# A tuned attention-and-experts kernel on one core: row remainders loaded in parts, and set issue times for the loads of later batches

## The chip, the cores and the metric

The kernel runs on one core of one Trainium2 chip. The metric is the device time of one execution in microseconds (us). The kernel before takes 508.6 us. All outputs are right. In each run the device time is about 1.8 us more than the span of its profile (508.58 against 506.8, say), so times are compared with times and spans with spans.

Engines are named as in the profile: PE is TensorE's matmuls, PEld its weight loads, ACT is ScalarE, DVE is VectorE, POOL is GpSimd and SP is SyncE. The program gives each of the five a queue of instructions of its own, and semaphores in it hold an instruction back until its inputs are there.

## The reference

Linear attention for 8 batches of 8 heads (576 rows, 64 columns), then a mixture of 4 experts on the 4608 rows that come out.

```python
phi(x) = np.where(x > 0, x, np.exp(x) - 1.0) + 1.0
q_p, k_p = phi(q), phi(k)                      # (8, 8, 576, 64)
kv  = einsum('bhsd,bhde->...', k_p, v)         # summed over the rows
z   = sum(k_p, axis=2)
x   = (q_p @ kv) / (q_p . z + 1e-06)           # then (4608, 512)
p   = domain_probs / (domain_probs.sum(-1) + 1e-9)
out = sum over e of  p[:, e] * (relu(x @ w1[e]) @ w2[e])   # D 512, F 1024
```

(The first two einsums are shortened to what matters here.)

## The kernel before

576 rows are 4 x 128 + 64. The 64 rows left over, the *row remainders*, are loaded for all heads of a batch at once. Attention goes by *pairs* of heads: `kv` sums over the rows of k and v, so it needs the remainders of k and v, but the outputs of the first 512 rows do not need the remainder of q.

The first 512 rows of batch 0 are run through the experts plainly as the weights arrive (the *ramp*, up to about 85 us). The other 4096 rows are 64 *units*, each 14 products of 8 or 4 matmuls, among which the attention of batches 2 to 7 is mixed in (until about 400 us).

The order of every engine's queue is made by a small planner inside the kernel. It goes through an assumed time line, takes on each engine the ready operation with the lowest `pri` (on POOL the next one as the program lists them), and writes the queues in the order found. A load lands, so the planner assumes, 2.0 us plus a moving time after its issue. `after` is the earliest assumed time of an operation. It is no time on the chip: on the chip it only settles where an instruction stands in its queue.

```python
    # Plan.order()
    start[n] = max(t, at[n])                  # at[n] begins as the operation's "after"
    free[e] = done = start[n] + o["dur"]
    if o["move"]:                             # a DMA
        mover = max(done + 1.2, mover) + o["move"]
        done = mover + 0.8                    # assumed landing
    ...
    def load_rest(b, queue, pri):             # the remainders: k, v and q together
        for i, (t, o) in enumerate(((k, kqr[rs, 0]), (v, vr[rs]), (q, kqr[rs, 1]))):
            dma(queue, pri, o, t[b, :, NT:S]..., (("str", par, i),), 0.75, ...)

    def rest_maps(b, pe_mode, pri):           # one exponential for k and q
        pl.add("ACT", 1.05, pri, lambda: nc.scalar.activation(er[rs], kqr[rs], AF.Exp),
               r=(s_[0], s_[2]), w=ek)
        ...
    # the start
    load_pair(0, 0, "SP", 0)
    load_rest(0, "POOL", 0)
    load_pair(0, 1, "POOL", 0)
    load_w1(0, (0,))
    ...
    def batch(b):                             # batches 2 to 7, mixed into the units
        due = U(8 * (b - 1)) - 8              # U(n) = 84 + 6.4 n, the assumed start of unit n
        for pr in range(DC):
            t = due - (DC - pr) * 2 * TU
            load_pair(b, pr, "SP", t - 12)    # only a priority: goes as soon as its buffer is free
            if pr == 0:
                load_rest(b, "SP", t - 12)
                rest_maps(b, False, t - 6)
            attention(b, pr, False, t, 1.7)
```

## Time and profile before

508.58 us (median of 3 runs, 508.37 to 508.6). The profiled run itself took 510.41 us, 1.8 us more than that median.

| where | time TensorE loses, us |
|---|---|
| 0 to 12 us | 11.5 |
| 12 to 34 us | 11.5 |
| 34 to 85 us | 1.3 |
| 85 to 115 us | 3.9 |
| 115 to 450 us | 1.0 |
| after 500 us | 7.5 |

*Lost* is the length of the stretch less the time that its matmuls take at the spacing of an unhindered stream (0.216 us for 512 columns, 0.109 for 256, 0.056 for 128). In all, the matmuls need 472.0 of the 508.6 us, so TensorE is the bound and 36.6 us is all that any reordering could win. It is a better measure here than the busy share, since matmuls overlap: the view of windows has PE busy for 484.1 us of the first 508.

Busy time of each engine by stage, from the view of windows of the kernel before. After the stretch and its length come the engines' busy times with instruction counts, then the granted clock (1.00 is full), the mean busy share of the DMA engines and GB/s:

```profile
0.00:12.00 12.00, 1.54 (x10) 0.97 (x10) 6.20 (x19) 6.30 (x10) 10.04 (x20) 1.00 0.86 226
12.00:34.00 22.00, 17.39 (x98) 9.29 (x99) 16.66 (x51) 13.52 (x29) 14.98 (x23) 0.92 1.15 223
...
60.00:85.00 25.00, 25.00 (x139) 12.27 (x138) 21.33 (x49) 18.29 (x36) 1.44 (x3) 1.00 0.88 175
85.00:115.00 30.00, 28.31 (x360) 24.19 (x358) 26.93 (x69) 24.77 (x48) 0.00 (x0) 1.00 0.99 213
115.00:260.00 145.00, 144.80 (x1992) 137.37 (x1990) 131.84 (x344) 120.73 (x230) 0.00 (x0) 1.00 0.65 146
```

(No clock is on record before 21.5 us in this trace; the 1.00 of the first stretch rests on none.)

The start, from the timeline of the kernel before (start, length, engine, line, operation, output and inputs; in brackets the idle time before it and what ended it):

```profile
9.21 1.06 ACT L317 ACTIVATE ek<-kqr 64x1024 f16<-64x1024 f32 x1 [0.30 <-DMA kqr<-in_q_dram]
...
10.77 0.29 PE L403 MATMUL l2b<-vpr,kqpr 128*128 128x130 f16 x1 [4.99 <-DVE kqpr L315]
...
16.73 1.44 PE L537 MATMUL l1b<-s,w 128*128 128x512 f16 x3 [0.15 <-ACT s L532]
...
24.02 0.27 DVE L289 TENSOR_REDUCE prs<-p 128x32 f32<-128x128 f32 x1
...
26.89 0.64 PE L527 MATMUL l2b<-identh,x 128*128 128x128 f16 x4 [0.80 <-DVE x L440]
...
28.21 1.36 PE L537 MATMUL l1b<-s,w 128*128 128x512 f16 x3 [0.67 <-ACT s L532]
```

One exponential for both remainders starts at 9.21 us, when the q remainder has landed; TensorE waits 5 us for the mapped k remainder until 10.77. The first expert matmul comes at 16.73. The norm of the last pair stands behind the probabilities (from 24.02) on DVE, and the last chunk of the first layer starts at 28.21, after two idle spells.

```profile
kq<-in_q_dram SPq DMA_DIRECT2D x18, 256.0 KB, 3.1
...
kq<-in_k_dram SPq DMA_DIRECT2D x17, 256.0 KB, 3.2
```

Almost nothing: 1.2 us. A load goes out as soon as its buffer is free (at the issue of a q load 1.7 other transfers from SP are in flight on average, counted from the trace), and is there when its turn comes.

### The profile page before, as it was taken

To read this page: it belongs to the slowest core of one execution; us is meant where nothing else is said; L and a number is where in the kernel's file an instruction comes from. 1 tells how busy PE (TensorE), PEld (TensorE's weight loads), DVE (VectorE), ACT (ScalarE), POOL (GpSimd) and SP (SyncE) were. 2 spreads that over 40 slices of the span, in tenths; PEclk is the share of its full clock that TensorE was granted. 3 is DMA by queue.
4 is the path that set the end of the run, shared out by engine and by line. 5 is a ranking of instruction groups with operands and counts; after the bars stand their busy time and mean duration, and the time that the engine had idled before them with its cause. 6 is when DMAs were issued, how large, how long until landed. Compare 5 with 4: busy or idle time off the path is not lost.

```text
span 508.6 us, 14922 instructions
## 1 busy us (share of the span) xinstructions
PE 484.1 (95%) x6008; PEld 425.0 (84%) x6008; DVE 410.6 (81%) x1035; ACT 367.1 (72%) x685; POOL 42.6 (8%) x68
## 2 busy tenths in 40 slices
PE   1889999999999999999999999999999999999994
PEld 0534454889999999999999999999999999999993
DVE  5867897889998989898988989799868676666754
ACT  5636658887987699768977897778666766666640
POOL 8756500000000000000000000000000000000000
PEclk9989999999999999999999999999999999999999
DMA  8999988995775678555665565645322432323311
GB/s 233 227 232 225 262 164 188 234 201 136 162 182 120 138 145 177 121 137 129 175 112 136 124 147 141 108 113 105 95 43 75 54 84 44 84 48 80 51 35 43
DMA packets 124006, 67.51 MB, mean 133 GB/s; under 512 B 94480, under 2 KB 117776, under 8 KB 123936
## 3 DMA queue, kind: packets, MB, share of 16 engines
q1 hardware_dynamic: 115216, 51.79, 46.9%
q0 software_dynamic: 8720, 14.76, 13.7%
q8 instruction: 47, 0.77, 0.7%
q14 instruction: 23, 0.19, 0.1%
HBM read 45.16 MB, written 9.44 MB: 107 GB/s over the span
## 4 chain that ended last, share of the span: by engine, by line
PE 85%; ACT 5%; DMA 4%; DVE 2%; issue 2%; POOL 0%; POOLq 0%; DVEq 0%; ACTq 0%
PE l1b L689 37%; PE l2b L765 36%; PE l2b L547 4%; PE l1b L537 4%; DMA kq<-in_k_dram 2%; PE at L424 2%; PE at L400 1%; DMA kqr<-in_q_dram 1%; ACT xp L649 1%; ACT ek L358 1%; DMA w<-in_moe_w_dram 1%; ACT h L703 1%; ACT l1b L706 1%; ACT p L706 0%; DVE x L440 0%
## 5 line engine op out<-in xcount | busy, mean ns | idle before, releaser
L689 PEld LDWEIGHTS <-w 128*128 128x128 f16 x2048 | 132.9, 98 | 5.6 <-issue 1.0
L765 PE MATMUL l2b<-w,h 128*128 128x256 f16 x768 | 115.1, 273 | 0.3 <-ACT h L703 0.2
L765 PE MATMUL l2b<-t,s 128*128 128x256 f16 x768 | 112.6, 273 | 0.0
L703 ACT ACTIVATE h<-l1b 128x512 f16<-128x512 f32 x128 | 76.7, 599 | 43.1 <-PE l1b L689 41.1
L689 PEld LDWEIGHTS <-w1x 128*128 128x128 f16 x1536 | 100.1, 98 | 5.5 <-issue 2.1
L765 PEld LDWEIGHTS <-s 128*128 128x128 f16 x1024 | 91.2, 98 | 7.1 <-DVE s L751 0.2
L709 DVE CUSTOM_DVE_ANT_0 h<-l1b,p 128x512 f16<-128x512 f32 x64 | 44.2, 691 | 50.1 <-PE l1b L689 48.5
L689 PE MATMUL l1b<-xT,w 128*128 128x128 f16 x1024 | 78.1, 219 | 0.8 <-ACT l1b L706 0.7
L689 PE MATMUL l1b<-xs,w1x 128*128 128x128 f16 x1024 | 77.9, 219 | 0.9 <-DVE h L709 0.4
L689 PE MATMUL l1b<-xs,w 128*128 128x128 f16 x1024 | 78.0, 219 | 0.0
L649 ACT ACTIVATE xp<-x,p_nat 128x512 f16<-128x512 f16 x112 | 76.6, 724 | 0.7 <-DMA xT<-xp 0.6
L765 PEld LDWEIGHTS <-h 128*128 128x128 f16 x768 | 67.3, 98 | 5.4 <-ACT h L703 0.9
L751 DVE TENSOR_TENSOR s<-h 128x512 f16<-128x512 f16 x128 | 53.8, 421 | 1.6
L706 ACT COPY u<-l1b 128x512 f32<-128x512 f32 x64 | 37.5, 586 | 16.0 <-PE l1b L689 15.8
L709 DVE CUSTOM_DVE_ANT_0 h<-l1b,u 128x512 f16<-128x512 f32 x64 | 43.7, 682 | 0.8 <-ACT h L703 0.5
L706 ACT COPY l1b<-l1b 128x512 f32<-128x512 f32 x64 | 36.8, 575 | 10.4 <-PE l1b L689 9.6
L706 ACT COPY p<-l1b 128x512 f32<-128x512 f32 x64 | 37.3, 583 | 7.9 <-PE l1b L689 6.7
L667 DVE TENSOR_TENSOR xs<-xT,xs 128x256 f16<-128x256 f16 x128 | 37.0, 289 | 5.1 <-PE l1b L689 0.5
L358 ACT ACTIVATE ek<-kq 128x512 f16<-128x512 f32 x60 | 37.8, 631 | 3.3 <-DMA kq<-in_k_dram 2.3
L689 PE MATMUL l1b<-xT,w1x 128*128 128x128 f16 x512 | 39.0, 219 | 0.0
L765 PE MATMUL l2b<-w,s 128*128 128x256 f16 x256 | 38.4, 273 | 0.0
L537 PE MATMUL l1b<-s,w 128*128 128x512 f16 x124 | 31.1, 399 | 1.4 <-ACT s L532 1.2
(99 smaller groups left out, 561.0 us busy)
## 6 DMA issues: line engine op xcount, KB each, us to landing
w<-in_moe_w_dram POOLq DMA_DIRECT2D x32, 256.0 KB, 7.3
out_dram<-ot SPq DMA_DIRECT2D x16, 512.0 KB, 2.8
kq<-in_k_dram SPq DMA_DIRECT2D x25, 256.0 KB, 3.3
vs<-in_v_dram SPq DMA_DIRECT2D x25, 256.0 KB, 2.9
kq<-in_q_dram SPq DMA_DIRECT2D x25, 256.0 KB, 3.2
kq<-in_k_dram POOLq DMA_DIRECT2D x5, 256.0 KB, 7.2
vs<-in_v_dram POOLq DMA_DIRECT2D x5, 256.0 KB, 6.6
kq<-in_q_dram POOLq DMA_DIRECT2D x5, 256.0 KB, 6.0
```

The costliest lines, as they stand in the source:

```text
L358: pl.add("ACT", 0.55, pri + i * step, lambda i=i: nc.scalar.activation(ek[:, i], kq[:, i], AF.Exp), r=(sk[i],), w=(("ek", ei, i),))
L424: nc.tensor.matmul(out=nds[u][c - c0], lhsT=qT[:, c] if c < C else qTr[par][:, pr], rhs=kvz, start=True, stop=True,)
L537: nc.tensor.matmul(out=bank, lhsT=w1_sb[e][:, dc, fj * P : (fj + 1) * P], rhs=xt0[:, dc, :], start=(dc == 0), stop=(dc == DC - 1),)
L547: nc.tensor.matmul(out=bank, lhsT=hts[ht[fj]][:, c * P : (c + 1) * P], rhs=w2_sb[e][:, fj, :], start=(fj == 0), stop=(fj == FC - 1),)
L649: pl.add("ACT", 0.55, pri, lambda c=c, src=src, ps=ps: nc.scalar.activation(xp[:, c, :], src, AF.Copy, scale=ps), r=r, w=(("xp", xi, c),))
L667: lambda o=o, a=a, b_=b_: tt(out=o, in0=a, in1=b_, op=AO.subtract),
L689: nc.tensor.matmul(out=bank[:, fc * P : (fc + 1) * P], lhsT=wt[:, kc, fc * P : (fc + 1) * P], rhs=r[:, kc, :], start=(start and fc == 0 an ...
L703: return lambda: nc.scalar.activation(o, bank, AF.Relu)
L706: return lambda: nc.scalar.copy(o, bank)
L709: return lambda: nc.vector._custom_dve(TENSOR_ADD_SAT, out=o, in0=bank, in1=t, s0=BIG, s1=0.0)
L751: pl.add("DVE", 0.36, U(n + 1) + d - 0.5, lambda i=i, a=a, b_=b_, alu=alu: tt(out=s4[:, i], in0=a, in1=b_, op=alu), r=r, w=(Q(i),))
L765: nc.tensor.matmul(out=l2b[bank][:, half * HD : (half + 1) * HD], lhsT=a[:, c, :], rhs=w[:, c], start=(opens and first and c == 0), stop=( ...
```

## The change

Its intent: start TensorE earlier by taking the q remainder of batch 0 out of the first pairs' way, and keep loads of later batches from going out long before they are needed. The diff, cut to its core:

```diff
-    def load_pair(b, pr, queue, pri):
+    def load_pair(b, pr, queue, pri, after=0.0):
...                                  # dma(..., after=after) hands it to the planner
-    def load_rest(b, queue, pri):
+    def load_rest(b, queue, pri, after=0.0, parts=(0, 1, 2)):
-    def rest_maps(b, pe_mode, pri):
+    def rest_maps(b, pe_mode, pri, parts=(0, 1)):
+        for i in parts:              # k and q each with an exponential of its own
+            pl.add("ACT", 0.55, pri + i * 0.5, lambda i=i: nc.scalar.activation(
+                er[rs, i], kqr[rs, i], AF.Exp), r=(sk,), w=(ek,))
+    def rest_late(pri):              # batch 0: q remainder turned, multiplied, normed for all pairs
...
-    load_rest(0, "POOL", 0)
+    load_rest(0, "POOL", 0, parts=(0, 1))
...
-    rest_maps(0, True, 3)
+    rest_maps(0, True, 3, (0,))
     for pr in range(DC):
         if pr == 3:
             load_pair(0, 3, "POOL", 0)
             load_w1(0, (2, 3))
+            load_rest(0, "POOL", 0, parts=(2,))
             probs()
...
+    rest_maps(0, True, 30, (1,))
+    rest_late(32)
...
         for pr in range(DC):         # in batch(b), for batches 2 to 7
             t = due - (DC - pr) * 2 * TU
-            load_pair(b, pr, "SP", t - 12)
+            if b == 2:
+                t = T0 + 4 + 10.5 * pr
+            load_pair(b, pr, "SP", t - 8, after=t - 8)
             if pr == 0:
-                load_rest(b, "SP", t - 12)
-                rest_maps(b, False, t - 6)
-            attention(b, pr, False, t, 1.7)
+                load_rest(b, "SP", t - 7, after=t - 7)
+                rest_maps(b, False, t - 2)
+            attention(b, pr, False, t, 1.5)
```

Left out: two more kv buffers for batch 0, laid with the identity matrix into a buffer that is free until the first unit's output.

More of the change, by code (lines that the diff above doesn't have):

```diff
@@ L147, in sb @@
         return pc.tile(shape, dt, tag=name, name=name)
-    identh = sb("identh", [P, P], FP16)
     w1_sb = [sb(f"w1_{e}", [P, DC, F], FP16) for e in range(E)]
@@ L182 @@
     xr_sb = sb("xr_sb", [P, B // 2, Dm], FP16)
+    s15h = s15.rearrange("p a d -> p (a d)").bitcast(FP16)
+    identh = s15h[:, 0:P]
+    kvs += [
+        s15h[:, P + i * 2 * DE : P + (i + 1) * 2 * DE].rearrange("p (h e) -> p h e", h=2)
+        for i in range(2)
+    ]
     kqs.append(
@@ L220, with dma @@
     last = {}
-    def dma(queue, pri, out_, in_, w, move, r=(), hold=False, mark=False):
+    def dma(queue, pri, out_, in_, w, move, r=(), hold=False, mark=False, after=0.0):
         eng = nc.gpsimd if queue == "POOL" else nc.sync
@@ L247, in dma @@
             move=move,
+            after=after,
         )
     stage = {}
-    def load_pair(b, pr, queue, pri):
+    def load_pair(b, pr, queue, pri, after=0.0):
         hs = slice(2 * pr, 2 * pr + 2)
@@ L258, in load_pair @@
         for t, o, key in ((k, kqs[i][:, 0], kk[0]), (v, vss[i], kk[2]), (q, kqs[i][:, 1], kk[1])):
-            dma(queue, pri, o, t[b, hs, 0:NT].rearrange("h (p c) d -> p h c d", c=C), (key,), 0.7, hold=b == 2)
-    def load_rest(b, queue, pri):
+            dma(queue, pri, o, t[b, hs, 0:NT].rearrange("h (p c) d -> p h c d", c=C), (key,), 0.7,
+                hold=b == 2, after=after)
+    def load_rest(b, queue, pri, after=0.0, parts=(0, 1, 2)):
         par = b % 2
         rs = slice(par * R, par * R + R)
-        for i, (t, o) in enumerate(((k, kqr[rs, 0]), (v, vr[rs]), (q, kqr[rs, 1]))):
-            dma(queue, pri, o, t[b, :, NT:S].rearrange("h s d -> s h d"), (("str", par, i),), 0.75, hold=b in (2, 3))
+        for i in parts:
+            t, o = ((k, kqr[rs, 0]), (v, vr[rs]), (q, kqr[rs, 1]))[i]
+            dma(queue, pri, o, t[b, :, NT:S].rearrange("h s d -> s h d"), (("str", par, i),), 0.75,
+                hold=b in (2, 3), after=after)
     def load_w1(e, dcs):
@@ L308, in rest_maps @@
         er = ek_b[ei].rearrange("p i h c d -> p i (h c) d")
-        ek = (("ek", ei, 0), ("ek", ei, 1))
-        s_ = [("str", par, i) for i in range(3)]
         def maps(i):
@@ L315, in maps @@
             nc.vector.tensor_tensor(out=o, in0=er[rs, i], in1=o, op=AO.min)
-        pl.add("ACT", 1.05, pri, lambda: nc.scalar.activation(er[rs], kqr[rs], AF.Exp),
-               r=(s_[0], s_[2]), w=ek)
-        pl.add("ACT", 0.55, pri + 0.1,
-               lambda: nc.scalar.copy(vprs[par][rs, :, 0:D], vr[rs]), r=(s_[1],), w=(("vpr", par),))
-        for i, key in enumerate(("kpr", "qpr")):
-            pl.add("DVE", 0.92, pri + 0.5, lambda i=i: maps(i), r=(s_[0], s_[2]) + ek, w=(key,))
+        for i in parts:
+            sk, ek, key = ("str", par, 2 * i), ("ek", ei, i), ("kpr", "qpr")[i]
+            pl.add("ACT", 0.55, pri + i * 0.5, lambda i=i: nc.scalar.activation(
+                er[rs, i], kqr[rs, i], AF.Exp), r=(sk,), w=(ek,))
+            if i == 0:
+                pl.add("ACT", 0.55, pri + 0.1, lambda: nc.scalar.copy(
+                    vprs[par][rs, :, 0:D], vr[rs]), r=(("str", par, 1),), w=(("vpr", par),))
+            pl.add("DVE", 0.92, pri + 0.5 + i * 0.5, lambda i=i: maps(i), r=(sk, ek), w=(key,))
         if not pe_mode:
@@ L326, in rest_maps, with turn, mm, norm @@
                 r=("qpr",), w=[("qTr", par, i) for i in range(DC)], move=1.2)
+    def rest_late(pri):
+        rs = slice(0, R)
+        def turn():
+            for pr in range(DC):
+                nc.tensor.transpose(
+                    out=tbank[:, pr * R : (pr + 1) * R],
+                    in_=kqpr[rs, 1, 2 * pr : 2 * pr + 2].rearrange("p h d -> p (h d)"),
+                    identity=identh[rs, rs],
+                )
+        pl.add("PE", 0.22, pri, turn, r=("qpr", "ident"), w=("l2b3",))
+        pl.add("DVE", 0.3, pri, lambda: nc.vector.tensor_copy(
+            qTr[0][:, :, rs], tbank[:, 0 : DC * R].rearrange("p (a t) -> p a t", a=DC)),
+            r=("l2b3",), w=[("qTr", 0, pr) for pr in range(DC)])
+        for p0, n in ((0, 3), (3, 1)):
+            ri = rot("rc", 2)
+            def mm(p0=p0, n=n):
+                for pr in range(p0, p0 + n):
+                    nc.tensor.matmul(
+                        out=slot[pr - p0], lhsT=qTr[0][:, pr], rhs=kvs[pr], start=True, stop=True
+                    )
+            def norm(p0=p0, n=n, ri=ri):
+                nd = at[rs, 0 : n * 2 * DE].rearrange("p (c h e) -> p c h e", c=n, h=2)
+                rc = rc_b[ri][rs]
+                nc.vector.reciprocal(rc[:, 0:n], nd[:, :, :, D:DE])
+                nc.vector.tensor_tensor(
+                    out=xr_sb[rs, 0, p0 * P : (p0 + n) * P].rearrange(
+                        "p (c h d) -> p c h d", c=n, h=2
+                    ),
+                    in0=nd[:, :, :, 0:D],
+                    in1=rc[:, 0:n].broadcast_to([R, n, 2, D]),
+                    op=AO.mult,
+                )
+            prs = range(p0, p0 + n)
+            pl.add("PE", 0.06 * n, pri + 1, mm,
+                   r=[("qTr", 0, pr) for pr in prs] + [("kvz", pr) for pr in prs], w=("at",))
+            pl.add("DVE", 0.25 + 0.16 * n, pri + 1.5, norm, r=("at",),
+                   w=[("xr", 0, pr) for pr in prs])
     def attention(b, pr, pe_mode, pri, step, two=False):
@@ L344, in attention @@
         vp = vps[vi]
-        zi = rot("kvz", 2)
+        zi = pr if two else rot("kvz", 2)
         kvz = kvs[zi]
@@ L372, in turn @@
                     )
+                if two:
+                    return
                 nc.tensor.transpose(
@@ L377, in turn @@
                 )
-            pl.add("PE", 0.32, pri + 3 * step, turn, r=(("kqp", pi, 1), "qpr", "ident"),
-                   w=(tk,))
+            pl.add("PE", 0.32, pri + 3 * step, turn,
+                   r=(("kqp", pi, 1), "ident") + (() if two else ("qpr",)), w=(tk,))
             pl.add("ACT", 0.5, pri + 3.5 * step, lambda: nc.scalar.copy(
                 qT.rearrange("p c t -> p (c t)"), tq[:, 0:NT]), r=(tk,), w=(("qT", ti),))
-            pl.add("DVE", 0.2, pri + 3.5 * step, lambda: nc.vector.tensor_copy(
-                qTr[par][:, pr, rs], tq[:, NT : NT + R]), r=(tk,), w=(("qTr", par, pr),))
+            if not two:
+                pl.add("DVE", 0.2, pri + 3.5 * step, lambda: nc.vector.tensor_copy(
+                    qTr[par][:, pr, rs], tq[:, NT : NT + R]), r=(tk,), w=(("qTr", par, pr),))
         else:
@@ L434, in norm @@
             if two and u:
-                nd = l2b[2][:, 2 * DE : 6 * DE]
+                nd = l2b[2][:, 2 * DE : (2 + 2 * n) * DE]
             nd = nd.rearrange("p (c h e) -> p c h e", c=n, h=2)
@@ L445, in norm @@
             )
-            if c0:
+            if n == 2:
                 nc.vector.tensor_tensor(
@@ L452, in norm @@
                 )
-        for u, (c0, n) in enumerate(((0, 3), (3, 2))):
+        for u, (c0, n) in enumerate(((0, 3), (3, 1 if two else 2))):
             ri = rot("rc", 2)
             pl.add("PE", 0.06 * n, pri + (5 + u) * step, lambda u=u, c0=c0, n=n: nd_mm(u, c0, n),
-                   r=(("qT", ti), ("qTr", par, pr), ("kvz", zi)), w=ndk[u])
-            pl.add("DVE", (0.72, 0.74)[u], pri + (5.5 + u) * step,
+                   r=(("qT", ti), ("kvz", zi)) + ((("qTr", par, pr),) if n == 2 else ()), w=ndk[u])
+            pl.add("DVE", (0.5, 0.74, 0.72)[n - 1], pri + (5.5 + u) * step,
                    lambda u=u, c0=c0, n=n, ri=ri: norm(u, c0, n, ri), r=ndk[u],
                    w=[("x", par, pr, c) for c in range(c0, min(c0 + n, C))]
-                   + ([("xr", b, pr)] if u else []))
+                   + ([("xr", b, pr)] if n == 2 else []))
     out_t = [
@@ L798, in l2_unit @@
         pl.add("ACT", 0.5, p0 + 3.5, lambda: nc.scalar.copy(
-            s15.rearrange("p a d -> p (a d)"), l2b[0]), r=("l2b0",), w=("s15",))
+            s15.rearrange("p a d -> p (a d)"), l2b[0]), r=("l2b0",),
+            w=("s15", "ident", ("kvz", 2), ("kvz", 3)))
         pl.add("DVE", 0.62, p0 + 4.5, lambda: tt(
@@ L829 @@
     pl.add("DVE", 0.8, 5, lambda: consts(1), w=(("vp", 1), ("vpr", 1), ("kvz", 1)))
+    pl.add("DVE", 0.4, 5, lambda: [nc.vector.memset(kvs[i], 0.0) for i in (2, 3)],
+           w=(("kvz", 2), ("kvz", 3)))
     for i in range(2):
```

## The prediction

> **What bounds it now.** TensorE. Summing matmuls at the warm spacing the timeline shows (512 columns 0.216 us, 256 columns 0.109, 128 columns 0.056) gives about 472 us of work in a span of 508.6 us. So only about 37 us can be won, and the page of stages and the timeline say where they lie: about 11 us are lost before 12 us, 11.5 more between 12 and 32 us, next to nothing from 32 to 85 us (matmuls back to back), 3.7 us between 85 and 115 us, 1 us from there to 500 us, and 9 us at the end (last output additions and store).
>
> **Start, before.** All of k, v, q remainders of batch 0 come first on the POOL queue: they land at 6.6, 7.6 and 9.1 us. One exponential covers k and q (1.06 us, from 9.21), so the k side waits for the q remainder; TensorE sits 5.0 us until 10.77 for the mapped k. The first turned x reaches the expert's first layer at 16.73. The last pair's norm stands in VectorE's order behind the probabilities (24.0 to 26.1); TensorE idles, and the last chunk starts at 28.21. The clock record shows half rate from 28.3 to 31.7 us (matmuls 0.43 us apart instead of 0.216). The Trainium skill (TensorE: Matmul & The Clock Gate, Part 1) gives such spells about 3.4 us; this trace agrees.
>
> **What the change removes, adds, moves.** The q remainder's load moves behind the last pair and w1: following loads move up some 0.7 to 1.0 us (issue 0.69 us). The k exponential shrinks from 1.06 to about 0.6 us and starts at 6.6 instead of 9.2. Pair 0 then waits for its own q (landed 8.25), not the remainder: I estimate the first x about 2.5 us earlier. From the four pairs it removes, on VectorE, 4 copies of 0.19, 4 xr products of 0.27 and a map of 0.85 (about 2.7 us) and small transposes on TensorE, and does nearly the same amount in one batch later, at about 25 to 35 us, where VectorE is under 60% busy. TensorE's total work is unchanged.
>
> **How much is critical.** From 28 to 87 us TensorE is gapless, and weights land 8 to 11 us before use (w2 of expert 0 by 26.0, used at 34.2; w1 of expert 1 by 31.0, used at 41.1), so a start up to some 6 us earlier carries through. I expect 3 to 5 us in the ramp, including perhaps 1.7 us if the second half-clock spell goes. Against it, VectorE is 81 to 91% busy from 60 to 90 us and may give back part.
>
> **Other batches' loads.** Set issue times, and batch 2's attention 5 to 12 us later, take ScalarE and VectorE work out of 85 to 100 us, where TensorE loses 2.8 us. I expect 1 us (from -1 to 2).
>
> **Predicted:** 503.2 us, range 499.0 to 507.0. Faster by over 2%: 0.07; within 2%: 0.91; slower by over 2%: 0.02.
>
> **Right if** the profile shows mapped k remainder by about 8 us, the first expert matmul at 13.5 to 15 us, the last chunk of the first layer at 23 to 26 us, no half-clock spell after 25 us, the first unit's matmuls at 82 to 85 us instead of 87.3, less lost from 85 to 115.
>
> **Wrong if** the fixed in-order queues stall on the late q remainder, the planner still puts the probabilities before the last norm, weights or VectorE's sums become the limit at 60 to 90 us, or batch 2's later x comes after its deadline near 130 us and TensorE waits there.

## More of the kernel before

From 115 us on PE is busy all the time, and DVE is at 91% (131.84 of 145), ACT at 83%. These two carry the units' evictions and the mixed-in attention together, with little to spare.

What ACT waited for between 115 and 400 us in the kernel before, from the view of waits (in total, times, longest), and its loads in that stretch from the view of DMA issues (KB of each, median us to landing):

```profile
ACT xp L649 <- DMA xT<-xp: 0.6, 2, 0.4
ACT ek L358 <- DMA kq<-in_k_dram: 0.6, 2, 0.4
```

## The result, and the profile after

511.19 us (median of 4 runs, 509.45 to 511.43), against 508.59 us for the kernel before on the same chip. The ratio is 1.0043, with a 95% interval from 1.002 to 1.0066: slower by 0.4%, small but clear of noise. The prediction had 503.2, from 499.0 to 507.0.

The start moves as predicted, though by less at the first expert matmul. The timeline of the kernel after:

```profile
6.42 0.63 ACT L327 ACTIVATE ek<-kqr 64x512 f16<-64x512 f32 x1 [2.23 <-DMA kqr<-in_k_dram]
...
8.37 0.27 PE L460 MATMUL l2b<-vpr,kqpr 128*128 128x130 f16 x1 [0.15 <-ACT vpr L330]
...
15.45 1.44 PE L594 MATMUL l1b<-s,w 128*128 128x512 f16 x3 [0.29 <-ACT s L589]
...
24.12 0.81 PE L594 MATMUL l1b<-s,w 128*128 128x512 f16 x3 [0.67 <-ACT s L589]
```

The k remainder's own exponential starts at 6.42 us, TensorE multiplies with the mapped k remainder at 8.37 instead of 10.77, the first expert matmul comes at 15.45 instead of 16.73, and the last chunk at 24.12 instead of 28.21. So 2.4 us are won at the k remainder, but 1.3 at the first expert matmul: from 7.63 to 15.45 us the chain of the kernel after runs on ACT (exponentials, casts and copies) for 6.4 of 7.8 us. The stages of the kernel after, in the view of windows:

```profile
0.00:12.00 12.00, 2.64 (x19) 1.84 (x20) 6.92 (x23) 6.77 (x12) 10.36 (x20) 1.00 0.88 241
12.00:34.00 22.00, 19.04 (x114) 9.85 (x112) 17.02 (x45) 13.25 (x28) 15.56 (x23) 1.00 1.18 222
...
60.00:85.00 25.00, 24.18 (x161) 12.82 (x160) 20.18 (x45) 15.49 (x31) 0.18 (x1) 1.00 0.59 116
85.00:115.00 30.00, 29.43 (x405) 27.48 (x403) 26.22 (x70) 25.14 (x51) 0.00 (x0) 1.00 0.73 171
115.00:260.00 145.00, 140.66 (x1904) 131.11 (x1902) 125.34 (x330) 117.15 (x223) 0.00 (x0) 1.00 0.65 142
```

TensorE has more done before 34 us (21.68 us busy instead of 18.93), and 85 to 115 us is better filled. From 115 to 260 us it is worse: 140.66 us busy of 145 instead of 144.80, and DVE and ACT did less in that stretch too. So it is not that one of these engines had more to do there. In *lost* time: 21.4 us before 115 us, where the kernel before had 28.1; but 8.2 us from 115 to 450 us, where it had 1.0.

What ended the idle time of PE and ACT there, from the view of waits of the kernel after, 115 to 400 us:

```profile
ACT ek L412 <- DMA kq<-in_q_dram: 3.7, 5, 2.0
...
PE at L481 <- DMA qT<-kqp: 2.0, 2, 1.2
ACT ek L412 <- DMA kq<-in_k_dram: 1.8, 3, 0.8
ACT vp L408 <- DMA vs<-in_v_dram: 1.7, 3, 0.6
...
PE l1b L746 <- ACT l1b L763: 0.8, 3, 0.3
PE l1b L746 <- DMA xT<-xp: 0.8, 1, 0.8
```

ACT now waits for loads: with a remainder's and a transpose's wait (0.6 and 0.3 us, not shown) it is 8.1 us instead of 1.2. TensorE's own waits in this view are 4.7 us: 2.8 end with a transpose (three waits, for transposes that took 5.9 to 6.2 us), 1.6 with ACT and 0.3 with DVE. So late transposes are a second path to TensorE beside ACT's queue. The landing of loads in the kernel after, same stretch:

```profile
kq<-in_k_dram SPq DMA_DIRECT2D x20, 256.0 KB, 3.1
...
kq<-in_q_dram SPq DMA_DIRECT2D x20, 256.0 KB, 3.9
```

k, v and q of a pair now go out in one burst, since all their buffers have been free for long when the set time comes. At the issue of a q load 3.0 other transfers from SP are in flight on average instead of 1.7 (counted from the trace), and it lands after 3.9 instead of 3.1 us. The longest took 6.2 us. What one such load does, in the timeline of the kernel after:

```profile
250.23 0.47 SPq L232 DMA_DIRECT2D kq<-in_q_dram  x1
...
250.80 1.19 SPq L443 DMA_TRANSPOSE qT<-kqp  x1
...
255.17 0.60 PE L822 MATMUL l2b<-w,h 128*128 128x256 f16 x4
...
256.43 0.63 ACT L412 ACTIVATE ek<-kq 128x512 f16<-128x512 f32 x1 [1.96 <-DMA kq<-in_q_dram]
...
256.98 0.34 PE L481 MATMUL at<-kvz,qT 128*128 128x130 f16 x3 [1.21 <-DMA qT<-kqp]
257.08 0.60 ACT L760 ACTIVATE h<-l1b 128x512 f16<-128x512 f32 x1
...
257.71 0.57 ACT L763 COPY l1b<-l1b 128x512 f32<-128x512 f32 x1
...
258.33 0.61 PE L746 MATMUL l1b<-xs,w1x 128*128 128x128 f16 x8
```

The q load issued at 250.23 lands at 256.41 us. The exponential that reads it (L412) stands in ACT's queue in front of the relu (L760) and the copy of the bank (L763). None of these two needs the load, but ACT takes its queue in order, so they come 2 us late, and the matmul at 258.33 waits for that copy. At the same time the transpose issued at 250.80, right behind the burst, takes until 256.93, and TensorE idles 1.21 us for it. The two delays overlap: only some 0.1 us of idle time is left before the matmul at 258.33, but without the late transpose it would still have waited for the copy. Nor was the burst alone on the way: k and v had landed by 252.95, and the transpose and, from 252.09, a store of output were in flight with q.

### The profile page after: what moved, and what is told of

Read it like the earlier page. It is cut to its first block, busy times and chain, and to the rows that moved or that the text cites. A ratio compares the mean times of both kernels' runs of the same rounds, so it can differ in the third digit from the quotient of the medians.

```text
span 509.2 us, 14848 instructions
## 1 busy us (share of the span) xinstructions
PE 483.3 (95%) x6008; PEld 424.1 (83%) x6008; DVE 409.5 (80%) x1034; ACT 368.4 (72%) x693; POOL 42.5 (8%) x68
## 4 chain that ended last, share of the span: by engine, by line
PE 72%; ACT 9%; DMA 7%; DVE 6%; issue 3%; SPq 1%; POOL 0%; DVEq 0%; POOLq 0%; ACTq 0%
PE l1b L746 29%; PE l2b L822 29%; PE l1b L594 6%; PE l2b L604 5%; DMA kq<-in_q_dram 2%; ACT xp L706 1%; ACT ek L412 1%; PE at L481 1%; DMA kqr<-in_q_dram 1%; ACT h L760 1%; DMA qT<-kqp 1%; DVE h L766 1%; DMA vr<-in_v_dram 1%; SPq L232 1%; ACT l1b L763 1%
## 5 line engine op out<-in xcount | busy, mean ns | idle before, releaser
L760 ACT ACTIVATE h<-l1b 128x512 f16<-128x512 f32 x128 | 76.6, 599 | 50.2 <-PE l1b L746 48.9
L763 ACT COPY u<-l1b 128x512 f32<-128x512 f32 x64 | 37.5, 585 | 16.1 <-PE l1b L746 15.7
L763 ACT COPY l1b<-l1b 128x512 f32<-128x512 f32 x64 | 36.7, 574 | 10.9 <-PE l1b L746 9.9
L763 ACT COPY p<-l1b 128x512 f32<-128x512 f32 x64 | 37.4, 585 | 8.2 <-PE l1b L746 5.6
L412 ACT ACTIVATE ek<-kq 128x512 f16<-128x512 f32 x60 | 37.8, 630 | 7.4 <-DMA kq<-in_q_dram 3.7
L405 DVE TENSOR_TENSOR kqp<-ek,kqp 128x512 f16<-128x512 f16 x64 | 27.2, 425 | 7.3 <-ACT ek L412 2.9
```

The lines of the kernel that those rows point to most:

```text
L405: nc.vector.tensor_tensor(out=o, in0=ek[:, i], in1=o, op=AO.min)
L412: pl.add("ACT", 0.55, pri + i * step, lambda i=i: nc.scalar.activation(ek[:, i], kq[:, i], AF.Exp), r=(sk[i],), w=(("ek", ei, i),))
L760: return lambda: nc.scalar.activation(o, bank, AF.Relu)
L763: return lambda: nc.scalar.copy(o, bank)
```

## The experiments

Twelve kernels ran, in three jobs; each job ran the kernel before in the same rounds (7 runs each: medians 508.58, 508.54 and 508.69 us), and each kernel has 4 runs. The rows *before* and *after* are from the change's own job. The last two columns are lost TensorE time in the profiled run, before 115 us and from 115 to 450 us.

| kernel | median us | range | ratio (95% interval) | lost before 115 | lost 115 to 450 |
|---|---|---|---|---|---|
| before | 508.6 | 508.4 to 508.9 | 1 | 28.1 | 1.0 |
| after | 511.19 | 509.45 to 511.43 | 1.0043 (1.0020 to 1.0066) | 21.4 | 8.2 |
| e1 ramp only | 507.25 | 506.97 to 507.59 | 0.9972 (0.9957 to 0.9988) | 25.3 | 0.9 |
| e2 batches only | 513.84 | 513.13 to 514.56 | 1.0101 (1.0081 to 1.0122) | 24.4 | 8.6 |
| e3 ramp, batch 2 moved | 505.82 | 505.58 to 506.79 | 0.9948 (0.9927 to 0.9969) | 23.1 | 1.3 |
| e4 no set times | 505.97 | 505.76 to 508.37 | 0.9957 (0.9931 to 0.9984) | 22.4 | 2.1 |
| e5 lead 16 us | 504.46 | 503.46 to 505.22 | 0.9913 (0.9892 to 0.9934) | 21.8 | 2.1 |
| e6 staggered | 509.00 | 508.50 to 509.46 | 1.0003 (0.9981 to 1.0024) | 21.2 | 6.5 |
| e7 planned late | 507.63 | 507.29 to 509.13 | 0.9983 (0.9960 to 1.0005) | 20.6 | 5.4 |
| e8 no set times, units from 80 | 504.76 | 504.66 to 504.93 | 0.9921 (0.9904 to 0.9937) | 21.6 | 2.0 |
| e9 lead 12 us | 507.06 | 506.42 to 508.36 | 0.9970 (0.9945 to 0.9996) | 21.1 | 4.0 |
| e10 lead 24 us | 504.89 | 503.54 to 505.48 | 0.9921 (0.9896 to 0.9945) | 20.8 | 3.2 |
| e11 lead 16, planned late | 504.17 | 504.04 to 504.34 | 0.9910 (0.9887 to 0.9932) | 22.1 | 0.7 |
| e12 lead 16, units from 80 | 505.35 | 504.15 to 505.48 | 0.9928 (0.9906 to 0.9950) | 20.8 | 3.3 |

(In the columns of losses, kernels that share the start of the change differ by up to 1.8 us before 115 us, so a single one of those numbers is not worth more than that. Part of it goes with the clock: in these twelve traces the first full clock is on record between 17.2 and 20.6 us, and the loss from 12 to 34 us rises with that time, from 6.5 to 7.9 us.)

### Which part costs the time: e1, e2, e3, e4

**e1** takes the changed kernel with `batch()` of the kernel before:

```diff
-            if b == 2:
-                t = T0 + 4 + 10.5 * pr
-            load_pair(b, pr, "SP", t - 8, after=t - 8)
+            load_pair(b, pr, "SP", t - 12)
             if pr == 0:
-                load_rest(b, "SP", t - 7, after=t - 7)
-                rest_maps(b, False, t - 2)
-            attention(b, pr, False, t, 1.5)
+                load_rest(b, "SP", t - 12)
+                rest_maps(b, False, t - 6)
+            attention(b, pr, False, t, 1.7)
```

> The changed kernel with the first part alone: remainders in parts and the q side finished late, but the other batches' loads and attention placed as in the kernel before. Theory T (the set issue times of the later batches' loads cost the time): the ramp's 5 us gain carries through, 502 to 505 us. Rival R (a start 5 us earlier only runs into ScalarE, VectorE or the transfers between 120 and 260 us, whatever the loads' times): 507 to 511 us.

Measured: 507.25 us. Neither theory had it. The rival's range holds the number, but its mechanism is absent: only 0.9 us are lost after 115 us. The ramp gains in the end 1.3 us, not 5. Where the rest went is seen before 115 us. Its profile has the last chunk early as in the change, but loses 2.3 us between 60 and 85 us (the kernel before 0.4 there). And one wait of 2.3 us follows at the first units, in the view of PE's waits of e1, 85 to 115 us:

```profile
PE l1b L746 <- DVE xs L724: 2.3, 1, 2.3
```

There DVE, 81 to 91% busy from 60 to 90 us in the kernel before, had become the limit. In sum: by 34 us e1 has lost 4.2 us less than the kernel before (18.8 against 23.0); 1.3 of these a kernel with the old start can gain too (e2, below), and 1.9 are lost again between 60 and 85 us. That leaves 1.0 us, near the 1.3 us measured.

**e2** is the kernel before with `after` in its loading helpers and `batch()` of the change, its start untouched.

```diff
-            load_pair(b, pr, "SP", t - 12)
+            if b == 2:
+                t = T0 + 4 + 10.5 * pr
+            load_pair(b, pr, "SP", t - 8, after=t - 8)
...                                  # load_rest, rest_maps and the step as in the change
```

> The kernel before with the second part alone: set issue times, batch 2 moved, new steps; the start unchanged. Theory T: slower than before, 511 to 517 us, with the new waits on SyncE transposes and late loads between 120 and 260 us. Rival R: about as before, 506 to 509 us, since without the earlier start nothing is run into.

Measured: 513.84 us, as the theory said, with 8.6 us lost after 115 us, and ACT again waiting for loads. From the view of waits of e2, 115 to 400 us (here L355 copies v and L707 copies banks):

```profile
ACT vp L355 <- DMA vs<-in_v_dram: 3.6, 5, 1.7
...
PE l1b L690 <- ACT l1b L707: 2.6, 4, 1.0
```

So the earlier start is not what upsets the later stages (rival R): they are upset without it.

e2 also shows a flaw in what the prediction read off a single trace. Up to 68 us its instructions are those of the kernel before, in the same order on every engine (compared from the two traces). The windows view from 26 to 34 us, first the kernel before, then e2:

```profile
26.00:34.00 8.00, 6.46 (x25) 2.58 (x25) 5.27 (x13) 4.30 (x8) 3.95 (x6) 0.79 1.18 206
```

```profile
26.00:34.00 8.00, 6.62 (x32) 2.81 (x31) 6.59 (x15) 4.93 (x9) 4.28 (x6) 1.00 1.18 207
```

The granted clock is 0.79 in one and 1.00 in the other. The half-clock spell from 28.3 to 31.7 us that I counted as 1.7 us to be won belonged to that profiled run. The same instructions may go without it, and e2 has lost 1.3 us less by 34 us. The Trainium skill (TensorE: Matmul & The Clock Gate, What's actually happening) says of the number of slow matmuls at a start that it varies from run to run, as the window that decides is free-running. At the start this pair differs a little (first full clock on record at 21.5 and 21.1 us, before the 57th and the 56th matmul); the spell at 28 us comes later than the start that the page speaks of. Of the fourteen traces here only that of the kernel before has it. Its profiled run was 1.8 us above the median, which fits. For the runs without a profile only the mean clock of the whole span is on record: of the 21 of the kernel before in the three jobs, three are as low as the profiled run's 0.994, among them the two slowest (510.23 and 510.26 us). So the spell seems to be rare, and the medians hold little of it.

**e3** is e1 with batch 2 placed as in the change:

```diff
             t = due - (DC - pr) * 2 * TU
+            if b == 2:
+                t = T0 + 4 + 10.5 * pr
             load_pair(b, pr, "SP", t - 12)
```

> As the first run, but batch 2 placed as in the change (pairs 10.5 us apart from 88 us on), with no set times and later batches as before. Theory T: at or below the first run, 500 to 503 us, since TensorE's losses from 85 to 115 us shrink by about 2 us. Rival B (moving batch 2 into 118 to 150 us is what upsets the later stages): 507 us or more, with the wait on transposes near 140 and 150 us.

Measured: 505.82 us, 1.4 us better than e1, with 1.3 us lost after 115 us. The 500 to 503 us hoped for was too low because the ramp had been oversized, but the step from e1 to e3 has the right sign and about the expected size (2 us). Moving batch 2 is a gain (the runs of e1 and e3 do not overlap), so rival B falls.

**e4** is the change without its lower bounds, all else the same:

```diff
-            load_pair(b, pr, "SP", t - 8, after=t - 8)
+            load_pair(b, pr, "SP", t - 8)
-                load_rest(b, "SP", t - 7, after=t - 7)
+                load_rest(b, "SP", t - 7)
```

> The changed kernel with the lower bound on the loads' issue times taken away and nothing else: same priorities, batch 2 moved, same steps. Theory T: most of the 7 us lost after 120 us comes back, 501 to 504 us. Rival S (the narrower steps and later remainder maps order ScalarE badly): 508 us or more.

Measured: 505.97 us, 5.2 us better than the change, though 2 us above what I expected, for the same reason as e3. ACT's waits for DMA between 115 and 400 us are 0.5 us instead of 8.1. From the view of waits of e4, which holds no other wait of ACT for a DMA and none other of PE:

```profile
PE l1b L746 <- ACT l1b L763: 0.7, 2, 0.5
ACT xp L706 <- DMA xT<-xp: 0.5, 1, 0.5
```

Narrower steps and later remainder maps (rival S) cost nothing visible: e4 has them and equals e3, which has not.

In steps, each the difference of two neighbours: 508.6 - 1.3 (ramp, e1) - 1.4 (batch 2 moved, e3) + 0.1 (steps and priorities, e4) + 5.2 (set times) = 511.2 us. Another order would give other sizes: without the new ramp the rest costs 5.3 us (e2 against the kernel before), with it 3.9 (the change against e1).

### Why set times cost: e5, e6, e7

Two theories for these. L: the loads have too little lead before their work is due. P: the plan puts the first reader where it assumes the load to land, and three loads sent together land later than assumed.

**e5** doubles the lead and leaves the burst:

```diff
-            load_pair(b, pr, "SP", t - 8, after=t - 8)
+            load_pair(b, pr, "SP", t - 8, after=t - 16)
-                load_rest(b, "SP", t - 7, after=t - 7)
+                load_rest(b, "SP", t - 7, after=t - 15)
```

> The changed kernel with the set times 8 us earlier (16 and 15 us ahead of the pair instead of 8 and 7), so k, v and q still go out together but earlier. Theory L (the loads have too little lead before TensorE's need): most comes back, 505 to 508 us. Theory P (the planned order of the engines puts each first reader at the load's assumed landing, whatever the lead, and three loads sent together land later than assumed): stays at 509 to 512 us, ScalarE still waiting about 8 us for loads between 115 and 400 us.

Measured: 504.46 us, better than any kernel so far. Theory P in the form that lead does not matter is refuted. The burst is still there: a q load finds 2.8 transfers in flight and lands later still. From the view of DMA issues and that of waits of e5, 115 to 400 us:

```profile
kq<-in_q_dram SPq DMA_DIRECT2D x19, 256.0 KB, 4.3
```

```profile
ACT ek L412 <- DMA kq<-in_q_dram: 1.7, 3, 1.3
```

Slow landing by itself does not hurt, then, if there is other work that the plan can put in between.

**e6** sends k, v and q 2.5 us apart:

```diff
+        for n_, (t, o, key) in enumerate(...):     # k, v, q
-                hold=b == 2, after=after)
+                hold=b == 2, after=after + 2.5 * (n_ - 1) if after else 0.0)
```

> The changed kernel with k, v and q of a pair set 2.5 us apart around the same mean time (v at the same time as in the change). Theory P with the burst as the cause: loads in flight at a q load fall from 3 to below 2, its landing from 3.9 to about 3.2 us, and the time to 506 to 508 us. Theory L: no gain, 510 to 513 us, as q leaves later still.

Measured: 509.00 us, between the two theories, and the edit missed its aim: a q load still finds 3.0 transfers in flight on average and lands after 4.2 us. That is 2.2 us better than the change, with ACT's waits for DMA at 6.8 us. It does not tell the theories apart, and says nothing about bursts.

**e7** leaves issue times and bursts, and tells only the planner that these loads land 2.5 us later. Readers move back in their queues:

```diff
-                done = mover + 0.8
+                done = mover + 0.8 + o["lag"]      # lag = 2.5 where a load has a set time
```

> The changed kernel with the same set times and bursts, but the planner told that these loads land 2.5 us later than it assumed, so that their readers are placed later in each engine's order. Theory P: ScalarE's waits for loads fall from 8 us to under 3 between 115 and 400 us, and the time to 505 to 508 us. Theory L: slower or the same, 510 to 513 us, since the work moves even nearer to its need.

Measured: 507.63 us, 3.6 us better than the change. ACT's waits for loads all but vanish. The view of waits of e7, 115 to 400 us, has only one of ACT's, and two of PE's for transposes:

```profile
PE l1b L747 <- DMA xT<-xp: 1.0, 1, 1.0
...
PE at L482 <- DMA qT<-kqp: 0.7, 1, 0.7
...
ACT vp L409 <- DMA vs<-in_v_dram: 0.6, 1, 0.6
```

The work did move nearer to its need, and by theory L alone this should have been slower. So both count at 8 us of lead: 3.6 us for readers that stand in the queue where the plan wrongly takes the load to be there, and some 3.5 us more that only more lead gives back (507.63 to 504.17 in e11 below, which is e7 but for the lead).

### How much lead: e9, e10, and with both remedies e11

> The changed kernel with the set times 12 and 11 us ahead of the pair instead of 8 and 7. If lead is what counts (theory L), between the change and the 16 us run: 506 to 509 us. If only a threshold matters, at 511 or at 504.5 us already.

> The same with 24 and 23 us, about when the buffers come free anyway. Theory L: as the 16 us run or as the run without set times, 503.5 to 506 us. If 16 us won by keeping loads off something earlier, it is slower than the 16 us run by 1 us or more.

> 16 us of lead and the planner told that these loads land 2.5 us later. If the planned order at the assumed landing (theory P) is a cost of its own beside the lead, ScalarE's remaining 2.9 us of waits for loads fall under 1 and the time is 502.5 to 504 us; if lead already covers it, 504 to 505.5 us.

e9 and e10 have `after=t - 12` and `after=t - 24` (remainders one less); e11 is e5 with the `lag` of e7. With a lead of 8, 12, 16 and 24 us the times are 511.19, 507.06, 504.46 and 504.89 us. So lead is what counts, and about 16 us is enough; 16 and 24 us cannot be told apart (their runs overlap). ACT's waits for DMA from 115 to 400 us are 8.1, 4.5, 2.7 and 3.2 us with these leads: less, but not gone. e11 takes 504.17 us, the best of all and 0.9% below the kernel before, but not clearly below e5. The chain of waits of e11 from 115 to 400 us, shares by line:

```profile
by line: PE l1b L747 48.3%; PE l2b L823 47.2%; PE at L482 2.3%; PE at L458 1.7%; PE at L461 0.4%; issue 0.0%
```

This is nothing but TensorE: no load, no ACT, no DVE is on it. At 16 us the `lag` has little left to win (0.3 us, not clear of noise), although ACT's waits for DMA fall from 2.7 us to none.

One thing the account does not explain: set times with 16 or 24 us of lead are also better than no set times at all. e5 is 1.5 us and e10 1.1 us below e4, and their runs do not overlap with e4's. The two traces of e4 and e5 lose the same 2.1 us from 115 to 450 us, so the gain does not show there. Why is left open.

### Tries at a better version: e8 and e12

Since units now begin near 83 us, the plan's assumed start was moved (`T0, TU = 80.0, 6.4` for `84.0, 6.4`), in e4 (giving e8) and in e5 (giving e12).

> A try at a better version: no set times, and the plan's start of the units moved from 84 to 80 us, as the trace now has them begin near 82. If the losses between 60 and 95 us come from priorities laid out for a later start, 504 to 505.5 us; if not, 506 us as without it.

> A try at a better version: 16 us of lead and the plan's start of the units at 80 us instead of 84. The earlier try with 80 won 1.2 us without set times; here 503 to 504.5 us if the two gains add.

e8 takes 504.76 us, 1.2 us less than e4, as expected, but not for the reason given: the loss from 60 to 95 us, where it was to win, is 2.4 us instead of 2.8. e12 takes 505.35 us, no better than e5 with its 504.46: the gains do not add. Why not is left open; ACT's waits for DMA from 115 to 400 us are 5.0 us in e12 and 2.7 in e5. The version to keep is e11, or e5, which is simpler by the lag.

## Why the prediction was wrong

- **Bound, right.** TensorE bounds the kernel in every run, and gains and losses are its idle time.
- **Start, mechanism right, size wrong.** Mapped k remainder by about 8 us: 7.5. Last chunk between 23 and 26 us: 24.12. First unit between 82 and 85: 82.4. No half-clock spell after 25 us: none until the end, at 506.8, but e2 with the old start has none there either, so this point was met without being the change's doing. The first expert matmul came a little later than said (15.45, not before 15), on ACT's chain. But "I expect 3 to 5 us in the ramp" was the mis-sized term. On the times the ramp alone is worth 1.3 us (e1). Part of it, "perhaps 1.7 us if the second half-clock spell goes", was read from one profiled run and is absent in another with the same instructions (e2). Another part was given back between 60 and 90 us to DVE. The prediction named that as something that "may give back part", without a size.
- **Batch 2, size right, mechanism in part.** 1.4 us from e1 to e3, where 1 was expected for the whole of the loads. But "take ScalarE and VectorE work out of 85 to 100 us" held for VectorE alone, and by little: from e1 to e3 DVE's busy time there goes from 13.90 to 13.14 us and TensorE's one wait for its `xs` from 2.3 to 0.9 us, while ACT goes from 13.56 to 13.75 us. In the change against the kernel before both are busier there (ACT 13.82 instead of 12.02 us, DVE 13.82 instead of 13.52).
- **The other batches' loads, the step that failed.** "I expect 1 us (from -1 to 2)" credited set times and the new place of batch 2 together, and gave the set times no cost: no wait for a load held back appears in it. On top of the rest they cost 5.2 us (change against e4), so this step came to 3.9 us lost (e1 to the change) instead of 1 won. That is 4.9 us of the 8.0 between 503.2 and 511.2; the ramp, 1.3 instead of the middle of 3 to 5, is 2.7. The set times cut the lead of every pair's load from whenever a buffer came free to 8 us of planned time. The profile before showed why this was not free: ACT and DVE at 83 and 91% from 115 to 260 us, fitting attention in where it could, and 1.2 us of waits for loads. The lesson was in those lines. The change treats the loads' earliness as something to be trimmed, when it was slack.
- **What was named as a risk and was not it.** The weights did not become the limit, and the probabilities no longer stood before the last norm. Batch 2's later x made TensorE wait once, 0.3 us, before the matmul at 128.30 us by the timeline.

What stays open: how the 3.5 us that lead gives beyond e7 divide between TensorE's waits for transposes behind a burst (1.7 us in e7's lines above) and evictions in a worse order. No run takes the burst away and leaves the lead at 8 us; e6 tried and failed.

## What to carry to other kernels

In a statically ordered kernel, a load that goes out early is not waste but leaves the plan room (here 8 us of lead cost 5.2 us against no set times, though 16 us cost nothing): before you hold it back, look at how busy the engines are that read it, and at what else stands behind the reader in an in-order queue. If you do set issue times, try two or three leads (here 8, 12, 16 us gave 511, 507, 504.5 us), and plan with the landing times of the trace's slow loads rather than of the typical one. And compare a saving read from one trace with a second run of the same instructions before counting it, above all where the clock plays a part.

The Trainium skill (Perfetto Trace Analysis, Optimization Strategy) advises to find the gaps of the bounding engine and make what they wait for start sooner or finish faster. This case agrees for the start (gaps of 5.0 and 0.8 us before the matmuls at 10.77 and 26.89, both shortened) and adds the other half: what has no gap in its trace can be given one, here 1.0 to 8.2 us after 115 us.

## What the Trainium skill lacked or had wrong

- DMA: Bandwidth & Descriptors (Anatomy of one DMA) gives a time for one transfer on the GpSimd path, 2.0 us plus bytes over 436 GB/s, which by my estimate is 2.6 us for 256 KB. No load ran alone on that path here: with several in flight, loads of 256 KB from POOL before 20 us took 5.8 to 6.4 us in the median (kernel before). It gives no such line for the SyncE path, nor one for several in flight. Measured from SyncE: k, first of its burst, 3.1 us in the median, q with 3.0 others in flight 3.9 us, at most 6.2 us.
- The same page (Issuing engines are not separate DMA queues) says that all transfers share the 16 engines and interleave. This agrees with transposes that land late behind a burst, but it gives no size for the delay: a transpose of 128 x 512 fp16 within SBUF took 2.9 us in the median and 6.1 us in the one case shown; five others issued with three to five transfers in flight took 2.9 to 4.1 us, so the number in flight at the issue does not settle it.
- The same page (Rules for kernel authors) advises to issue a DMA early and wait on it late, for its setup cost. It gives no size for what holding a load back costs work that does not read it. Here set times with 8 us of lead cost 5.2 us, and 3.6 us came back when the readers were placed later in the in-order queues (e7).
- TensorE: Matmul & The Clock Gate (What's actually happening) says that slow matmuls vary from run to run. It does not say that a spell in mid-kernel can come and go with the same instructions: granted clock 0.79 in one run and 1.00 in another from 26 to 34 us.
